# A state-space mixer with an MLP gate: state at every token instead of every second one, D by diagonal products, half-row products, B transposed from HBM

## Chip, cores, metric

One core of a Trainium2 chip. The metric is the device time of one execution in microseconds (us): the median of the runs. Engines: TensorE (PE, its weight loads PEld), VectorE (DVE), ScalarE (ACT), GpSimd (POOL), and SyncE (SP), which issues transfers.

## The reference

The input x has 2048 tokens of 448 values. It is normalised, and the result goes two ways: a complex diagonal state-space layer (with a skip term D) and a normalised MLP with GELU. The MLP's result gates the first through SiLU. Cut to what matters:

```python
def _A_ref(x, Lambda_re, Lambda_im, B_re, B_im, C_re, C_im, log_dt, Dskip):
    dt = jnp.exp(log_dt)
    Lam_bar = jnp.exp(dt * Lam)
    B_bar = ((Lam_bar - 1.0) / Lam)[:, None] * Bmat
    Bu = jnp.einsum("bld,pd->blp", x + 0j, B_bar)
    for t in range(L):
        h = Lam_bar[None, :] * h + Bu[:, t, :]
    y = 2.0 * jnp.einsum("blp,dp->bld", hseq, Cmat).real + x * Dskip[None, None, :]
    return y
def _B_ref(x, w1, b1, w2, b2):
    y = _layernorm(x, axis=-1)
    h = _gelu(jnp.einsum("bsd,df->bsf", y, w1) + b1)
    return jnp.einsum("bsf,fd->bsd", h, w2) + b2
xn = _layernorm(x, axis=-1)
return x + _A_ref(xn, ...) * _silu(_B_ref(xn, ...))
```

L is 2048, the state has 448 complex values, the MLP 1792 hidden ones. Inputs and output are bf16.

## The kernel before

**Tiles.** The 2048 tokens are taken in four groups g of 512; a group has two blocks b of 256 tokens, and a block is held as 128 partitions with two tokens each (par 0 the even one, par 1 the odd one). Every group goes through the same steps.

**Norms.** `ln_stats`, `ln_scale` and `ln_apply` make two normalised copies (xn for the state-space layer, xm for the MLP); `xt` transposes them by DMA into `xnT` and `xn2T`, so that input dimensions lie on partitions.

**State, every second token.** The state is kept after each pair of tokens: NK = 256 steps a group. `bu` multiplies the transposed pair (896 inputs, seven chunks of 128) by `BT`, which holds B for the odd token and Lambda times B for the even one. `lb` builds Lambda times B from the loaded `Bn` (ACT or DVE scale, DVE combine), `bt` transposes the result by DMA. `ssm` then works on DVE: two products and an add with the sine and cosine table `WT` (lines 669 to 673) turn the complex recurrence into real scans (line 677, seven a group, decay R2 of two tokens); ACT copies the result to bf16 (`s_b`, 681 to 684); POOL carries the last state to the next group (`cur`, 691 to 703); two products and an add (705 to 709) turn the state back into `h_sb`. The state's tiles are three real, three imaginary and one mixed.

**Output tiles.** `ym` makes y. For the odd token: seven products of h with `CQ` (C times the input factor). For the even token: seven products of the state before the pair with `CZ` (C times Lambda times that factor) and four products of the input with `M0`, the direct matrix from x to y of the same token. `m0` multiplies `Bn` with `CQ` (631, 636), copies the result and adds D on its diagonal (644). For odd tokens D enters through `skip`, as `xd` (776) and `xr` (808). `cq` builds CQ and CZ with `combine` (590 to 593).

**MLP.** For group 0 `mm1_half` (746) multiplies whole 128-row chunks, the last padded with zeros and the bias row, 256 tokens at a time; for the other groups `mm1` (726) uses 64-row halves, so that two products share the array. ACT applies GELU (736, 752). `mm2` (760) makes the output, DVE adds b2 (763), ACT applies SiLU (764). Then DVE multiplies by the gate (810) and adds x (813), and SP stores the tile.

**Order.** Every step is a task in `Plan`; its dependencies come from the keys that it reads and writes. The order of all tasks is written out as a list of numbers and tags, `ORDER`; every engine runs its tasks in that order, one after another, and a wait stops all that stands behind it on that engine. Some tasks have two versions (`either`); those in the list `SECOND` take the second one. PSUM banks are fixed in the code.

Of the kernel before, what the change touches and what calls it, by code (L numbers as in the profile page):

```python
# [7 lines left out]
ACT = mybir.ActivationFunctionType  # L8
# [9 lines left out]
class Task:  # L18
# [3 lines left out]
    __slots__ = ("eng", "ins", "reads", "writes", "sem", "idx", "deps", "chain", "alts", "tag")  # L22

    def __init__(self, eng, ins, reads, writes, sem):
        self.eng, self.ins, self.reads, self.writes, self.sem = eng, ins, tuple(reads), tuple(writes), sem
        self.deps = set()
        self.chain = False
        self.tag = None
        self.alts = [(eng, ins)]

    def choose(self, k):
        self.eng, self.ins = self.alts[k]
        if self.sem in ENGS:
            self.sem = self.eng


class Plan:
# [4 lines left out]
    def __init__(self, nc):  # L42
        self.nc = nc
# [19 lines left out]

    def add(self, eng, ins, reads=(), writes=(), dur=0.2, lat=0.1, prio=0.0, sem=None, chain=False, table=None, mode=None):
# [3 lines left out]
        t.chain = chain  # L68
# [7 lines left out]
    def either(self, first, second, reads=(), writes=(), prio=0.0, chain=False):  # L76

        t = self.add(first[0], first[1], reads, writes, chain=chain)
        t.alts.append((second[0], second[1] if isinstance(second[1], list) else [second[1]]))
        return t  # L80

    def dma(self, eng, out_ap, in_ap, reads=(), writes=(), prio=0.0, nbytes=0, transpose=False, dur=0.45):
# [8 lines left out]
        return self.add(eng, fn, reads, writes, sem=sem)  # L91
# [20 lines left out]
    def emit(self):  # L112
# [5 lines left out]
        assert len(order) == len(set(order)) == len(self.tasks)  # L118
        done = {}
# [26 lines left out]

    def settle(self, names):
# [14 lines left out]
ST 0 18 22 10 88 1 19 16 23 15 20 2 21 11 3 9 27 12 26 24 8 17 14 13 25 5 7 6 89 4 28 90 96 91 29 45 30 97 92 98 93 31 46 47 94 99 48 63 103  # L162
95 32 53 100 49 54 101 50 102 33 51 52 114 64 44 106 65 55 38 108 116 56 105 115 39 107 57 109 40 117 58 118 41 120 42 119 36 110 122 34 121
111 37 144 124 35 104 123 43 60 112 62 125 59 B0 126 DH 72 113 67 B1 296 68 69 128 B2 70 127 300 298 73 B3 151 130 129 299 191 148 132 303
131 149 297 134 133 301 302 150 304 136 152 135 142 155 138 66 156 143 153 140 154 137 157 271 139 71 146 308 305 74 165 76 75 141 306 61
309 145 79 307 166 268 82 272 163 BF 83 77 310 86 169 164 181 158 277 269 159 401 180 400 270 170 167 398 147 160 274 W0 W1 W2 405 168 404
182 399 W3 171 280 402 403 183 161 406 172 H10 173 275 162 H11 192 278 184 281 356 174 H12 175 357 185 358 311 78 410 360 80 176 81 H13 361
312 411 229 407 412 408 362 230 409 501 502 H15 363 500 314 188 231 359 315 504 383 189 506 503 H16 232 505 507 508 H14 186 368 178 364 369
187 233 509 365 179 512 366 234 H21 513 177 237 316 H20 367 238 460 313 239 458 510 461 235 242 190 246 373 243 459 245 514 195 193 196 511
236 247 H24 244 H23 194 199 251 466 85 197 200 84 464 198 203 87 249 252 201 253 240 202 241 205 248 204 317 370 206 215 262 217 207 382 318  # L170
218 257 216 258 319 208 254 259 250 D0 263 255 260 209 320 371 256 264 321 210 219 221 D1 220 211 223 265 266 273 222 376 267 413 374 322
224 212 225 D2 326 276 213 227 226 379 325 279 228 214 D3 327 282 331 465 333 323 283 414 285 375 377 332 380 H26 415 334 467 H22 O00 335
470 324 484 462 471 328 289 330 284 416 339 329 286 340 463 261 341 342 H30 290 343 344 417 337 336 292 515 548 418 O01 345 H25 351 516 346
549 H31 485 347 287 348 468 288 293 349 H33 350 550 372 352 338 554 419 378 353 518 354 294 384 291 420 295 421 469 385 387 422 551 423 517
O10 555 388 574 391 389 424 519 428 386 427 475 392 429 437 394 435 425 520 472 426 390 430 436 431 521 432 476 473 481 522 438 O11 433 381
523 440 395 482 447 393 478 434 448 524 575 439 441 442 443 449 450 453 444 451 445 525 446 355 479 452 H32 526 454 H34 455 552 396 556 553
456 397 529 457 H36 557 H35 530 560 531 558 561 539 527 538 559 486 565 483 474 528 487 536 477 535 489 480 534 532 562 537 541 O20 566 533
540 493 488 542 563 544 567 490 564 568 491 494 492 543 545 496 569 546 571 570 O21 495 547 581 572 497 573 578 498 576 O30 499 577 582 579
583 580 584 585 593 589 586 594 595 587 588 590 591 596 592
""".split()]  # L180
SECOND = [int(k) if k.isdigit() else k for k in """
142 143 144 157 163 167 171 173 195 201 219 223 308 309 407 411 413 416 484 485 508 509 512 515 516 518 519 575 W0 W1 W2 595
""".split()]

# [10 lines left out]
def bass_recurrent_scan__ssm_conv_s5__mixer_channel_mlp__prompt_kernel(  # L195
# [14 lines left out]
    NB, NG, NF, NK = 8, 4, 14, 256  # L210
# [3 lines left out]
    with ExitStack() as es:  # L214
        def SB(name, shape, dtype=BF):
# [5 lines left out]
        iota = SB("iota", [128, NK], F32)  # L221
        sgn = SB("sgn", [128, 4], F32)
        cw = SB("cw", [128, 40, 4], F32)
# [3 lines left out]
        dcol = SB("dcol", [128, 8], F32)  # L227
        x_all = SB("x_all", [128, NB, 2, D])
        w1_sb = SB("w1_sb", [128, 4, F])
        w2_sb = SB("w2_sb", [128, NF, D])  # L230
        b1b = SB("b1b", [128, NF])
        b1f = SB("b1f", [128, NF], F32)
        Bn = SB("Bn", [128, 7, 896])
        BT = SB("BT", [128, 7, 7, 128])
        Cr = SB("Cr", [128, 7, D])
# [9 lines left out]
        o2 = SB("o2", [128, 4, D], F32)  # L245
        WT = SB("WT", [128, 4, 3, NK])
        xn_sb = SB("xn_sb", [128, 2, 896])
        xn2_sb = SB("xn2_sb", [128, 2, 1024])
        xnT = SB("xnT", [128, 2, 7, 256])
# [8 lines left out]
        pb = SB("pb", [128, 3, 2, NK])  # L258
        v_sb = SB("v_sb", [128, 4, 2, NK])
        s_f = SB("s_f", [128, 4, 2, NK], F32)  # L260
        s_b = SB("s_b", [128, 4, 2, NK])
        h_sb = SB("h_sb", [128, 2, 7, NK + 2])
        Cs = h_sb[0:112, 1, :, :].rearrange("p k c -> p (k c)")[:, 18:530]
# [8 lines left out]
        (LRE, LIM, LDT, DT, F1, A1, R1, R2, F2, DEN, RDEN, LR, LI, NLI, T0, T1, QR, QI, NQR, NQI, ZR, ZI, NZR, NZI,  # L272
         T2, ZT) = range(26)
# [4 lines left out]
        def pool(fn, reads=(), writes=(), dur=0.3, prio=0):  # L278
            kb.add("pool", fn, reads, writes, dur=dur, lat=0.15, prio=prio)

        def dve(fn, reads=(), writes=(), dur=0.2, prio=0):
            kb.add("dve", fn, reads, writes, dur=dur, lat=0.12, prio=prio)

        def act(fn, reads=(), writes=(), dur=0.6, prio=0, table=None):
            kb.add("act", fn, reads, writes, dur=dur, lat=0.2, prio=prio, table=table)

        def pe(fn, reads=(), writes=(), dur=0.2, prio=0):
            kb.add("pe", fn, reads, writes, dur=dur, lat=0.25, prio=prio)

        with nc.Block():  # L290

            S0 = -100
            kb.tag = "ST"
            dve(lambda e: e.memset(still[:], 0.0), [], ["still"], 0.1, S0)
            pool(lambda e: e.memset(ident[:], 1.0), [], ["ident"], 0.2, 3 * PINNED)
            pool(lambda e: e.affine_select(ident[:], ident[:], [[1, 128]], ALU.is_equal, 0.0, base=0,
                                           channel_multiplier=-1), ["ident"], ["ident"], 0.4, 3 * PINNED)
            pool(lambda e: e.memset(sgn[:], -1.0), [], ["sgn"], 0.1, S0)
            pool(lambda e: e.affine_select(sgn[:, 0:1], sgn[:, 0:1], [[0, 1]], ALU.is_ge, 1.0, base=63,
                                           channel_multiplier=-1), ["sgn"], ["sgn"], 0.2, S0)  # L300
            act(lambda e: e.preload_act_table_set("natural_log_exp_and_others"), [], ["warm"], 0.05, 5 * PINNED, "exp")
            pool(lambda e: e.iota(iota[:], [[1, NK]], base=0, channel_multiplier=0,
                                  allow_small_or_imprecise_dtypes=True), [], ["iota"], 0.6, S0)

            pool(lambda e: e.tensor_scalar(sgn[:, 1:2], sgn[:, 0:1], -TWO_PI, None, op0=ALU.mult), ["sgn"], ["sgn1"], 0.2, S0)
            pool(lambda e: e.tensor_scalar(sgn[:, 2:3], sgn[:, 0:1], TWO_PI, None, op0=ALU.mult), ["sgn"], ["sgn2"], 0.2, S0)
            pool(lambda e: e.memset(sgn[:, 3:4], math.pi / 2), ["sgn"], ["sgn3"], 0.1, S0)
            XN = ["xn0", "xn1"]
            XM = ["xm0", "xm1"]
            dve(lambda e: e.memset(vrows[:, 0:64], 0.0), [], ["vr"], 0.1, S0)  # L310
            dve(lambda e: e.memset(w1_sb[64:128, 3, :], 0.0), [], ["w1b"], 0.5, S0)
# [617 lines left out]
```

## Time and profile before

| | |
|---|---|
| median of 3 runs | 154.56 us (154.44 to 154.69) |
| profiled execution, first to last instruction (span) | 153.0 us |
| mean granted TensorE clock | 0.999 |
| busy: PE, DVE, ACT, POOL | 148.4, 122.0, 110.9, 34.8 us |
| HBM read and written | 6.20 MB, 1.84 MB |

The profile shows one execution. Its span leaves out what lies around the instructions, and the median of the runs is 1.56 us above it. A row of a group reads: line, engine, operation, output<-inputs, shapes, count | busy time, mean ns of one | idle time of the engine before it and what ended that. PE's group means contain the pipeline's latency; what a product costs in a stream is read from the chain of waits. Rows of the timeline give start, duration and line.

### The profile page before, as it was taken

To read this page: it belongs to the slowest core of one execution; us is meant where nothing else is said; L and a number is where in the kernel's file an instruction comes from. 1 tells how busy PE (TensorE), PEld (TensorE's weight loads), DVE (VectorE), ACT (ScalarE), POOL (GpSimd) and SP (SyncE) were. 2 spreads that over 40 slices of the span, in tenths; PEclk is the share of its full clock that TensorE was granted. 3 is DMA by queue.
4 is the path that set the end of the run, shared out by engine and by line. 5 is a ranking of instruction groups with operands and counts; after the bars stand their busy time and mean duration, and the time that the engine had idled before them with its cause. 6 is when DMAs were issued, how large, how long until landed. Compare 5 with 4: busy or idle time off the path is not lost.

```text
span 153.0 us, 2971 instructions
## 1 busy us (share of the span) xinstructions
PE 148.4 (97%) x1055; PEld 88.2 (58%) x1055; DVE 122.0 (80%) x262; ACT 110.9 (72%) x190; POOL 34.8 (23%) x115
## 2 busy tenths in 40 slices
PE   7899999999999999999999999999999999999992
PEld 2599965455555555665544456755666555555551
DVE  5785989998957999899898864494976972999564
ACT  3867769999959988699999999832294789661100
POOL 6467491073000060310004310210006000000241
PEclk9999999999999999999999999999999999999999
DMA  4999986999989770000020221131300100001022
GB/s 114 297 324 366 252 185 118 177 125 227 196 143 121 140 137 0 4 0 0 2 50 14 42 78 60 27 38 27 95 4 0 60 0 0 4 0 62 0 107 73
DMA packets 31512, 14.04 MB, mean 92 GB/s; under 512 B 25733, under 2 KB 31113, under 8 KB 31498
## 3 DMA queue, kind: packets, MB, share of 16 engines
q1 hardware_dynamic: 31344, 13.79, 40.1%
q8 instruction: 8, 0.13, 0.3%
q10 hardware_dynamic: 154, 0.07, 0.2%
q14 instruction: 6, 0.05, 0.1%
HBM read 6.20 MB, written 1.84 MB: 53 GB/s over the span
## 4 chain that ended last, share of the span: by engine, by line
PE 94%; DVE 2%; DMA 1%; issue 0%; DVEq 0%
PE psum L760 28%; PE psum L726 21%; PE psum L652 14%; PE psum L795 13%; PE psum L746 8%; PE psum L798 4%; PE psum L631 3%; DMA x_all<-in_A_x_dram 1%; PE psum L801 1%; DVE lnst L395 1%; PE psum L636 1%; PE psum L403 1%; PE psum L466 0%; DVE xn2T L407 0%; DVE t L810 0%
## 5 line engine op out<-in xcount | busy, mean ns | idle before, releaser
L760 PE MATMUL psum<-w_sb,gT 128*128 128x448 bf16 x224 | 44.5, 353 | 0.0
L726 PE MATMUL psum<-xn2T,w_sb 64*128 64x512 bf16 x294 | 33.5, 378 | 0.0
L760 PEld LDWEIGHTS psum<-w_sb,gT 128*128 128x128 bf16 x224 | 21.8, 98 | 19.5 <-issue 0.2
L736 ACT ACTIVATE gT<-psum,b1f 128x512 bf16<-128x512 f32 x42 | 25.9, 690 | 3.1 <-PE psum L726 3.1
L726 PEld LDWEIGHTS psum<-xn2T,w_sb 64*128 64x128 bf16 x294 | 15.6, 109 | 16.3 <-issue 2.3
L652 PE MATMUL psum<-xnT,BT 128*128 128x256 bf16 x196 | 24.1, 273 | 0.0
L652 PEld LDWEIGHTS psum<-xnT,BT 128*128 128x128 bf16 x196 | 18.5, 98 | 6.4 <-issue 3.1
L677 DVE TENSOR_TENSOR_SCAN s_f<-cw,cur,v_sb 128x256 f32<-128x256 f32 x21 | 15.1, 740 | 0.2
L451 ACT ACTIVATE xn_sb<-x_all,lnw 128x448 bf16<-128x448 bf16 (+1 forms) x21 | 13.4, 667 | 1.2 <-POOL lnw L428 1.2
L764 ACT ACTIVATE g_sb<-o 128x448 bf16<-128x448 f32 x16 | 8.9, 572 | 6.4 <-DVE o L763 6.2
L746 PE MATMUL psum<-xn2T,w_sb 128*128 128x256 bf16 x112 | 12.7, 273 | 0.4 <-DVE xn2T L407 0.4
L746 PEld LDWEIGHTS psum<-xn2T,w_sb 128*128 128x128 bf16 x112 | 11.9, 111 | 0.9 <-issue 0.8
L795 PE MATMUL psum<-CZ,h_sb 128*128 128x448 bf16 x56 | 11.9, 353 | 0.0
L810 DVE TENSOR_TENSOR t<-psum,g_sb 128x448 bf16<-128x448 f32 (+2 forms) x10 | 5.7, 574 | 7.6 <-PE psum L798 3.8
L656 ACT ACTIVATE u_sb<-psum 128x512 bf16<-128x512 f32 x12 | 7.1, 593 | 5.9 <-PE psum L652 5.8
L763 DVE TENSOR_TENSOR o<-psum,b2bc 128x448 f32<-128x448 f32 x16 | 9.7, 614 | 1.5 <-PE psum L760 1.5
L795 PE MATMUL psum<-CQ,h_sb 128*128 128x448 bf16 (+2 forms) x54 | 10.5, 332 | 0.0
L752 ACT ACTIVATE gT<-psum 128x512 bf16<-128x512 f32 x14 | 8.2, 593 | 3.2 <-PE psum L746 3.1
L381 DVE BATCH_NORM_STATS2 lnst<-x_all 128x6 f32<-128x448 bf16 x14 | 8.3, 610 | 0.6 <-DMA x_all<-in_A_x_dram 0.5
L590 ACT ACTIVATE tmp<-Cr,cw 128x448 f32<-128x448 bf16 (+1 forms) x12 | 7.9, 672 | 1.0 <-DVE CQ L593 0.9
L691 POOL TENSOR_TENSOR cwk<-s_f,ang 128x3 f32<-128x3 f32 x3 | 1.1, 352 | 32.6 <-DVE s_f L677 32.5
L795 PEld LDWEIGHTS psum<-CZ,h_sb 128*128 128x128 bf16 x56 | 5.4, 98 | 4.9 <-issue 0.4
(157 smaller groups left out, 212.0 us busy)
## 6 DMA issues: line engine op xcount, KB each, us to landing
out_dram<-tmp SPq DMA_DIRECT2D x7, 224.0 KB, 1.9
x_all<-in_A_x_dram SPq DMA_DIRECT2D x3, 448.0 KB, 4.5
w_sb<-in_B_w_dram SPq DMA_DIRECT2D x3, 448.0 KB, 6.6
w_sb<-in_B_w_dram SPq DMA_DIRECT2D x3, 384.0 KB, 4.6
Bn<-in_A_B_im_dram SPq DMA_DIRECT2D x1, 336.0 KB, 9.3
Bn<-in_A_B_re_dram SPq DMA_DIRECT2D x1, 336.0 KB, 9.8
x_all<-in_A_x_dram SPq DMA_DIRECT2D x2, 112.0 KB, 2.1
x_all<-in_A_x_dram SPq DMA_DIRECT2D x1, 224.0 KB, 3.7
```

The lines of the kernel that those rows point to most:

```text
L381: dve([lambda e, b=b, par=par, q=q: e.bn_stats(lnst[:, q, :], x_all[:, 2 * g + b, par, :])], [f"x{2 * g + b}"] + (["xmT0p1"] if (g, b) == ...
L451: ("act", [lambda e, o=o, i=i: e.activation(o, i, ACT.Identity, bias=nb, scale=rs) for o, i in pairs], 0.75, 0.2)]
L652: fns = [lambda e, r=r, m=m, d=d: e.matmul(psum[:, 4, r * NK:(r + 1) * NK], BT[:, m, d, :], xnT[:, gx, d, :], start=(d == 0), stop=(d == 6 ...
L677: dve(lambda e, i=i, ri=ri, init=init: e.tensor_tensor_scan(s_f[:, i, ri, :], col(R2, i).to_broadcast([128, NK]), v_sb[:, i, ri, :], init, ...
L726: return lambda e: e.matmul(psum[:, b0 + k, :], w1_sb[halves[h], d, fcol(2 * j + k)], rhs[halves[h], d, :, :], start=first and d == 0, sto ...
L736: act([lambda e, k=k: e.activation(gT[:, gb, 2 * j + k, :], psum[:, b0 + k, :], ACT.Gelu_apprx_tanh, bias=b1f[:, 2 * j + k:2 * j + k + 1]) ...
L746: fns = [lambda e, k=k, d=d: e.matmul(psum[:, banks[k], :].rearrange("p (r c) -> p r c", r=2)[:, :, cs], w1_sb[:, d, fcol(2 * j + k)], rhs ...
L752: act(lambda e: e.activation(gT[:, 0, 2 * j:2 * j + 2, :].rearrange("p k (r c) -> p k r c", r=2)[:, :, :, cs], psum[:, b0:b0 + 2, :].rearr ...
L760: fns = [lambda e, fi=fi: e.matmul(psum[:, bk, 0:D], gT[:, gb, fi, q * 128:(q + 1) * 128], w2_sb[:, fi, :], start=(fi == 0), stop=(fi == N ...
L763: dve(lambda e: e.tensor_tensor(o2[:, ob, :], psum[:, bk, 0:D], b2bc[:], ALU.add), [f"ps{bk}", "b2bc"], [f"oo{ob}"], 0.62, prio - 76)
L764: act(lambda e: e.activation(g_sb[:, gs, :], o2[:, ob, :], ACT.Silu), [f"oo{ob}"] + (["silu"] if g == 0 else []), [f"g{gs}"], 0.58, prio - ...
L795: fns = [lambda e, k=k: e.matmul(psum[:, bk, c0:c1], h_sb[:, hb, k, k0:k0 + 128], cm[:, k, c0:c1], start=(k == 0), stop=False) for k in ra ...
```

## The change

The state is kept at every token. NK becomes 512, the scans use the decay R1 of one token, and Lambda times B, CZ and M0 are gone with `lb`, `m0` and `skip`. A block's tokens are laid out as two runs r of 128 neighbours, and x and its normalised copies are padded to 512 columns (the last 64 twice), so that the input rows lie in two 64-row halves. `bu` and both forms of the first MLP product go through one function that issues 64-row products for two results in turn. D enters in `ym` by four products of the transposed input with diagonal tiles `DG`. B comes transposed from HBM (its last 64 columns by way of a small copy `Bs`). The bias b1 is transposed on PE from rows that ACT loads, and GELU takes it for group 0 too. The banks of PSUM are given by a list, `BANKS`, and the order is a new list. The add of x can run on DVE or POOL: by the new `SECOND` 13 of 17 such adds run on POOL (all of groups 0 to 2, one of group 3). The scaling for CQ runs on ACT alone, as does the absolute value of the table.

The core of the diff ("..." where lines are left out; `x_all[:, xa(...)]` is the new place of a token run):

```diff
-    NB, NG, NF, NK = 8, 4, 14, 256
+    NB, NG, NF, NK = 8, 4, 14, 512
...
-        CZ = SB("CZ", [128, 7, D])
-        M0 = SB("M0", [128, 4, D])
-        dbc = SB("dbc", [128, D])
-        xd = SB("xd", [128, 4, D])
-        xr = SB("xr", [128, 2, D], F32)
+        DG = SB("DG", [128, 4, 128])
...
+            for r in range(2):
+                ld("sp", x_all[:, xa(0, r), 0:D], dram_ap(A_x, r * 256 * D, [[D, 128], [1, D]]), [f"x0p{r}"], 114688)
+            ldw1(0)
+            ldx(1, 1)
...
+                for d in range(4):
+                    h = slice(0, 128) if d < 3 else slice(0, 64)
+                    n = 128 if d < 3 else 64
+                    pool(lambda e, d=d, h=h, n=n: e.tensor_scalar(DG[h, d, 0:n], ident[h, 0:n], dcol[h, d:d + 1], None, op0=ALU.mult),
+                         ["ident", "dcol", f"DG{d}"], [f"DG{d}"], 0.4)
...
+            def bt():
+                for k, (bm, row, n, at) in enumerate(((A_B_re, 0, 224, 0), (A_B_im, 0, 192, 512), (A_B_re, 224, 224, 224), (A_B_im, 192, 192, 704), (A_B_im, 384, 64, 448))):
+                    kb.dma("sp", BT[:, 0:3, at:at + n], dram_ap(bm, row * D, [[D, n], [1, 384]]), writes=[f"BT{k}"], nbytes=768 * n, transpose=True)
...
+                def half(k, d, h):
+                    first = h == k
+                    return lambda e: e.matmul(out(k), wt(k, d, halves[h]), rhs(k, d, halves[h]),
+                                              start=first and d == 0, stop=not first and d == 2)
+
+                own = [half(k, d, k) for d in range(4) for k in range(2)]
+                other = [half(k, d, 1 - k) for d in range(3) for k in (1, 0)]
+                kb.tag = tag
+                pe(own, rd, [bank.key], rows(4, n))
+                pe(other, rd, [bank.key], rows(3, n))
...
-                            s_f[:, i, ri, :], col(R2, i).to_broadcast([128, NK]), v_sb[:, i, ri, :], init, ALU.mult, ALU.add),
+                            s_f[:, i, ri, :], col(R1, i).to_broadcast([128, NK]), v_sb[:, i, ri, :], init, ALU.mult, ALU.add),
...
+                    fns = [lambda e, k=k: e.matmul(psum[:, bank.b, c0:c1], h_sb[:, hb, k, k0:k0 + 128], CQ[:, k, c0:c1], start=(k == 0), stop=(k == 6))
                            for k in range(7)]
+                    ds = [d for d in range(4) if c0 <= d * 128 < c1]
+                    fns[1:1] = [lambda e, d=d: e.matmul(psum[:, bank.b, d * 128:min(D, d * 128 + 128)], xnT[:, gx, r * 4 + d, xs], DG[:, d, 0:min(128, D - d * 128)],
+                                                        start=False, stop=False) for d in ds]
...
+                    on = [("dve", add, 0.15 + 0.25 * w / D), ("pool", add, 0.2 + 1.0 * w / D)]
+                    kb.either(*on, rd, [f"o{ob}_{r}_{c0}"])
```

The first transfers on SP are now, in the new order: the second run of block 0, the last piece of w1 (192 KB), the first run of block 0, block 1, and then the first piece of w1 (384 KB) and its last rows (loaded twice, into both halves). The order of the groups' work stays as before in its outline: the MLP of group 0 first, then input products, scans and MLP of the following groups side by side, output tiles as their states come.

More of the change, by code (lines that the diff above doesn't have):

```diff
@@ L145, in emit, with place @@
         self.settle(list(self.counts))
+    def place(self, order):
+        held = {b.key: b for b in self.banks}
+        for t in self.tasks:
+            for k in set(t.reads + t.writes):
+                if k in held:
+                    held[k].tasks.append(t)
+        for b, k in zip(self.banks, BANKS, strict=True):
+            b.b = k
+        now = {}
+        for t in order:
+            for k in t.writes:
+                b = held.get(k)
+                if b is None or now.get(b.b) is b:
+                    continue
+                for i in range(b.b, b.b + b.n):
+                    if i in now:
+                        t.deps.update(now[i].tasks)
+                    now[i] = b
     def settle(self, names):
@@ L166 @@
[L166 to L173, printed above, removed]
@@ L468, in xt @@
[L468 to L472 removed]
+                bank = kb.psum()
+                pe([lambda e, d=d: e.transpose(psh[:, bank.b, d * 128:(d + 1) * 128], src[:, b, d * 128:(d + 1) * 128],
+                                               ident[:, :]) for d in range(8)], [key, "ident"], [bank.key], rows(8))
@@ L831, in bass_recurrent_scan__ssm_conv_s5__mixer_channel_mlp__prompt_kernel @@
-            P = {"ln": -9, "bu": -8, "mm1": 0, "mm2": 5, "ym": 6}
-            def pr(k, g, x=0.0):
-                return P[k] + 10 * g + x
+                if r and not last:
+                    kb.dma("sp", dram_ap(out, off, [[D, 128], [256 * D, 2], [1, D]]), o_sb[:, ob, :].rearrange("p (r d) -> p r d", r=2),
+                           reads=[f"o{ob}_0_0", f"o{ob}_1_0", f"o{ob}_1_256"], writes=[f"out{g}{b}"], nbytes=229376)
+            idle = kb.psum()
+            kb.tag = "I0"
+            pe([lambda e: e.matmul(psum[:, idle.b, :], still[:, :], still[:, None, :].to_broadcast([128, 4, 128]), start=True, stop=True) for _ in range(8)],
+               ["still"], [idle.key], 3.4)
```

804 lines of the change are left out of this document (367 added, 437 removed).

## The prediction

> **What bounds the kernel now.** I read the page first: its busy times and slices.
>
> ```profile
> PE 148.4 (97%) x1055; PEld 88.2 (58%) x1055; DVE 122.0 (80%) x262; ACT 110.9 (72%) x190; POOL 34.8 (23%) x115
> PE   7899999999999999999999999999999999999992
> DVE  5785989998957999899898864494976972999564
> ```
>
> PE is full in every slice between the head and the tail; DVE is full in many slices up to the middle and has holes after it. A busy PE can still wait inside a group, so I read the chain of waits next: it names the work whose end set the next start.
>
> ```profile
> by line: PE psum L760 27.8%; PE psum L726 21.5%; PE psum L652 14.5%; PE psum L795 13.1%; PE psum L746 8.2%; PE psum L798 4.0%; PE psum L631 2.6%; DMA x_all<-in_A_x_dram 1.3%; PE psum L801 1.0%; DVE lnst L395 0.8%; PE psum L636 0.5%; PE psum
> ...
> 7.22 5.40 PE psum L746 x48
> 12.62 0.45 PE psum L466 x8
> ...
> 41.19 3.13 PE psum L726 x28
> ...
> 150.06 0.43 DVE t L810
> 150.59 0.42 DVE tmp L813
> ```
>
> From 7.22 to 150.06 us the chain stays on PE without a break: 142.8 us of products. So TensorE's own work bounds the kernel, with 7.2 us of head and 2.9 us of tail. The last row gives the tail behind DVE: it ends at 151.0 us of a span of 153.0, so 2.0 us go to the last store. The span is 153.0 us and the median of the runs 154.56; I add their difference, 1.56 us, to every span below.
>
> The chain's durations are also the true prices of products: 28 half-row products of 512 columns take 3.13 us (0.112 each), 48 full ones of 256 columns 5.40 us (0.112 each), eight of 128 columns 0.45 us (0.056 each).
>
> **The change, part by part: TensorE.** M0 is no longer built: L631 and L636, 3.1% of 153.0, go (-4.8 us). M0's products go too, L798 4.0% (-6.1). In their place each of the 16 output tiles gets four diagonal products of at most 128 columns: 64 x 0.056 = +3.6. The input product L652 (14.5%, 22.2 us) becomes 168 half-row products of 512 columns (18.8) and 56 of 256 columns, two of which share the array: 28 pairs x 0.112 = 3.1, together 21.9 (-0.3). The first MLP products of group 0, L746 (12.5 us), lose their padded rows: 98 pairs of half-row products of 256 columns x 0.112 = 11.0 (-1.5). Sum: -9.1 us.
>
> Here the pairs are the unknown, since no row has half rows with 256 columns. The weight loads must also run in pairs:
>
> ```profile
> L726 PEld LDWEIGHTS psum<-xn2T,w_sb 64*128 64x128 bf16 x294 | 15.6, 109 | 16.3 <-issue 2.3 <-ACT gT L736 0.6 <-ACT w_sb L851 0.4
> ```
>
> 294 loads of 109 ns would be 32 us one after another; they cover 15.6, so two do run at once. A pair then costs 0.112, as I took it; were they serial, a pair would cost 2 x 0.109 = 0.218 and 126 pairs 13.4 us more. The diagonal products could cost from 0.056 to a load's 0.109 each, +3.4 us at the worst; they are nearest to the eight of 0.056.
>
> The load order puts one weight piece before the second row block of x, and the first products need both halves of the last rows; I take 0.3 us later for the first product. A TensorE that never waits would give a span of 153.0 - 9.1 + 0.3 = 144.2.
>
> **VectorE: what it gains and loses.** Every step of the scan part now runs over 512 tokens in place of 256 pairs.
>
> ```profile
> L677 DVE TENSOR_TENSOR_SCAN s_f<-cw,cur,v_sb 128x256 f32<-128x256 f32 x21 | 15.1, 740 | 0.2
> L705 DVE TENSOR_TENSOR pa<-s_b,WT 128x1536 bf16<-128x1536 bf16 x4 | 3.8, 948 | 0.0
> L563 DVE SCALAR_TENSOR_TENSOR s_f<-iota,cw,s_f 128x256 f32<-128x256 f32 x4 | 1.7, 474 | 0.0
> L708 DVE TENSOR_TENSOR pa<-s_b,WT 128x512 bf16<-128x512 bf16 x4 | 1.7, 422 | 1.2 <-ACT s_b L684 1.2
> L566 DVE SCALAR_TENSOR_TENSOR s_f<-s_f 128x1024 f32<-128x1024 f32 x1 | 1.2, 1224 | 0.0
> L709 DVE TENSOR_TENSOR h_sb<-pa 128x256 bf16<-128x256 bf16 x4 | 1.2, 289 | 0.1
> ```
>
> From L708 to L705, 1024 more elements cost 0.526 us; so 1536 to 3072 elements cost 0.79 more, for 24 instructions +18.9. Eight of 512 elements go to 1024: 8 x 0.26 = +2.1; eight of 256 to 512, by L709 to L708: 8 x 0.13 = +1.1. The 28 scans have one length only. At least they grow by the slope of L563 to L566 (0.977 ns an element, 0.25 us: +7.0), at most they double (0.74: +20.7). I take off L563's fixed part of 0.22 and double the rest: 0.52 each, +14.6. The table's f32 steps grow by about 2.0, and L566 goes to ACT: +0.8. Added: 37.5 us.
>
> ```profile
> L593 DVE SCALAR_TENSOR_TENSOR Bn<-Bn,cw,tmp 128x448 bf16<-128x448 bf16 x7 | 4.7, 671 | 0.0
> L593 DVE SCALAR_TENSOR_TENSOR CZ<-Cr,cw,tmp 128x448 bf16<-128x448 bf16 x7 | 4.7, 679 | 0.0
> L591 DVE TENSOR_SCALAR tmp<-Bn,cw 128x448 f32<-128x448 bf16 (+1 forms) x4 | 1.8, 454 | 0.0
> L591 DVE TENSOR_SCALAR tmp<-Cr,cw 128x448 f32<-128x448 bf16 x4 | 1.8, 446 | 0.1
> L644 DVE SCALAR_TENSOR_TENSOR M<-ident,dcol,psum 128x128 bf16<-128x128 bf16 (+1 forms) x4 | 1.3, 332 | 1.0 <-ACT M L633 0.5 <-ACT M L638 0.4
> L776 DVE TENSOR_TENSOR xd<-xn_sb,dbc 128x448 bf16<-128x448 bf16 x7 | 2.7, 379 | 0.0
> L808 DVE TENSOR_TENSOR xr<-psum,xd 128x448 f32<-128x448 f32 x7 | 4.3, 611 | 2.9 <-PE psum L801 2.9
> L852 DVE COPY w_sb<-w_sb 64x512 bf16<-64x512 bf16 x3 | 0.9, 288 | 0.1
> L311 DVE MEMSET w_sb<- 64x896 uint32 x1 | 0.8, 805 | 0.2 <-issue 0.2
> L813 DVE TENSOR_TENSOR tmp<-t,x_all 128x448 bf16<-128x448 bf16 x15 | 6.3, 430 | 0.1
> L450 DVE TENSOR_SCALAR xn_sb<-x_all,lnw 128x64 bf16<-128x64 bf16 x6 | 1.8, 297 | 0.0
> ```
>
> All these go, but of L813's 15 adds two stay on DVE: by the new list of second choices 13 adds of x run on POOL. Removed: 24.8 without L813, and 13 x 0.43 minus 0.3 for a half tile that comes to DVE, 5.3: 30.1 us in 63 instructions. Durations overlap on DVE, so less is freed:
>
> ```profile
> 2.85 0.63 DVE L395 BATCH_NORM_STATS2 lnst<-x_all 128x6 f32<-128x448 bf16 x1 [0.42 <-DMA x_all<-in_A_x_dram]
> ...
> 13.10 0.69 DVE L472 COPY xn2T<-psum 128x1024 bf16<-128x1024 bf16 x1 [1.61 <-PE psum L466]
> ...
> 129.67 2.03 DVE L677 TENSOR_TENSOR_SCAN s_f<-cw,cur,v_sb 128x256 f32<-128x256 f32 x3
> ```
>
> Three scans of 0.740 take 2.03, so each begins 0.06 before the last one ends; with dependent ones I take 0.05, and 63 x 0.05 = 3.2 was never on the clock. DVE's busy time becomes 122.0 + 37.5 - (30.1 - 3.2) = 132.6 us.
>
> DVE is one queue, so its sum is a path: its first statistics at 2.85, waits of the head 2.2 (the 1.6 before L472 and an estimate of 0.6 for shorter ones), 132.6, the tail 2.0: 139.7, plus 2.0 as an estimate for waits on ACT's copies and on late products: 141.7. That is still below TensorE's 144.2.
>
> **The new collision: POOL's adds beside VectorE.** The trace has this case.
>
> ```profile
> 98.66 1.38 POOL L775 TENSOR_TENSOR xd<-xn_sb,dbc 128x448 bf16<-128x448 bf16 x1 [9.86 <-DVE xr L808]
> ...
> 144.62 1.09 POOL L775 TENSOR_TENSOR xr<-xd,g_sb 128x448 f32<-128x448 bf16 x1 [23.33 <-ACT g_sb L764]
> ```
> ```profile
> 99.18 1.10 DVE L813 TENSOR_TENSOR tmp<-t,x_all 128x448 bf16<-128x448 bf16 x1
> ...
> 145.39 0.80 DVE L810 TENSOR_TENSOR t<-xr,g_sb 128x448 bf16<-128x448 f32 x1
> ...
> 146.64 0.62 DVE L810 TENSOR_TENSOR t<-psum,g_sb 128x448 bf16<-128x448 f32 x1 [0.45 <-PE psum L798]
> ```
>
> The DVE add that began beside POOL's 1.38 took 1.10 and ended just after it; other adds take 0.38 when nothing is beside them, so it lost 0.72. The next, beside 1.09, lost 0.18 (0.80 against 0.62). In the new order most of POOL's 13 adds stand beside scans and wide products of two SBUF tensors. I take the mean loss, 0.45 each: +5.9. The ends are 0 and POOL's own 1.09, 14.2 together. On POOL itself the adds wait for their gated tiles, and behind them in its queue stand the products that carry a group's last state to the next group's scans; these have a group's time to spare, so I add nothing.
>
> The DVE path is then 141.7 + 5.9 = 147.6 us, above TensorE's 144.2: VectorE, not TensorE, sets the end, and the last state of group 3 comes about 3.4 us after TensorE could use it. What waits on it: the four output tiles of group 3, their gating and the last store.
>
> **The other engines.** ACT gains wider copies (u, s_b: twice the elements), two gelus in place of one for each tile of group 0, and the second halves of the tables; it loses the Bn and CZ scalings and the M0 copies. I estimate 122 us from 110.9, with at least 20 us of room beside DVE: no term. SP issues as many transposes (26), seven of B now from HBM or a small copy in place of the 7 of Bn, which saves the wait for LB; B is needed only after group 0's MLP, 20 us later: no term, up to 2 us if the transposes queue behind the late norm of group 0.
>
> Forecast: 147.6 + 1.56 = 149.1 us (149.16, taken as 149.1).
>
> **The rivals.**
> 1. TensorE stays full: POOL's adds fall into DVE's waits and cost nothing. For it: DVE's path without them, 141.7, is below 144.2. Against: only 2.5 us of room over the whole span. 144.2 + 1.56 = 145.8 us.
> 2. Slower: each POOL add stops VectorE for its whole length. 141.7 + 13 x 1.09 = 155.9, 157.4 us. It decides from a loss of 0.87 us an add, where the path reaches 153.0. For it: L813's 0.72 of a possible 0.86. Against: L810's 0.18, and adds that stand beside instructions that read PSUM (146.64, beside POOL's second one, took its usual 0.62). The Trainium skill (SBUF — State Buffer, section SBUF: two separate sides) says that the pair of ports that VectorE and GpSimd share is an exclusive lock held for the whole instruction, against DVE instructions with two SBUF inputs or in a two-port mode. By that rule this rival is the likely one; the L813 row agrees (0.72 lost), and the L810 row shows how little is lost where POOL is nearly done.
> 3. A cold TensorE. If the 3.4 us come as one wait, the clock may fall before the last tiles.
>
> ```profile
> 1.04 3.60 PE L837 MATMUL psum<-still 128*128 128x512 bf16 x8 [1.04 <-DVE still L294]
> ```
>
> At the start, eight products of 512 columns take 3.60 us, 0.45 each, twice the warm price. The last four tiles, about 6 us, would lose up to 3.4 us while it lasts: 152.5 us. The Trainium skill (TensorE: Matmul & The Clock Gate, section HAM oscillation) says that gaps of over some 3.4 us bring the half clock back; no row of before has such a gap.
> 4. Half rows of 256 columns don't share the array: 144.2 + 13.4 = 157.6, 159.2 us. The load row speaks against it.
>
> **How the numbers follow.** Chances: forecast 0.46 (own range 147.0 to 151.5, from a loss of 0.3 to 0.6 an add), TensorE full 0.22, the port rival 0.19, cold TensorE 0.06, half rows 0.03, something else late (B's transposes, ACT) 0.04. 0.2% of 154.56 is 0.3 us, about what a measurement of this kernel can tell from no change. Faster: 0.43 of the forecast, 0.22, 0.03 of the cold case, 0.02 of the rest, 0.70 in all. Slower: 0.02 of the forecast, 0.19, 0.02 of the cold case, 0.03, 0.01: 0.27. Same: what is left, 0.03. The range goes from 145.8 (TensorE full) to 156.3 (a loss of 1.0 an add: 141.7 + 13.0 + 1.56); it leaves out the half-row case, the upper half of the port rival and a little below 145.8, together under 0.2.
>
> **What would show it.** Right: DVE's busy time at 130 to 140 us and above 85% in every slice; PE near 140 with waits before group 3's output tiles; the chain of waits on DVE (scans, wide products) in the second half; wide products of 1.74 us, scans near 1.26; instructions beside POOL's adds longer by some 0.5. Wrong: scans above 1.4 or below 1.1; a chain that stays on PE to the end (rival 1); wide products of 2.5 us and more in number beside POOL's adds (rival 2); granted clock below 0.97 (rival 3); half-row products of group 0 above 0.075 each (rival 4).

## The result: slower by 7.7%, and the profile after

The changed kernel takes 168.74 us (median of 4 runs, 165.98 to 170.68), the kernel before 154.62 beside it: ratio 1.077, 95% interval 1.067 to 1.087. The forecast was 149.1, in a range of 145.8 to 156.3. Some executions lose a few us to a lower granted clock (and in one of a later kernel TensorE ran at half speed throughout), and the ratios are made without these, so a ratio can stand below what two medians give. By the ratio the changed kernel takes 166.5 us, 17.4 more than the forecast.

The page of the changed kernel's profile: busy times, then the slices of PE, DVE and the granted clock. This execution took 170.68 us, its span is 169.0.

```profile
PE 148.9 (88%) x1164; PEld 80.1 (47%) x1164; DVE 136.6 (81%) x195; ACT 123.7 (73%) x185; POOL 78.7 (47%) x119
PE   7736399999798999999499999999989999993892
DVE  2860069858599979989949999999998969999934
PEclk9999968999999999999969999999999999999579
```

DVE's total is near what was forecast, and from the second quarter on most of its slices are full, as they should be. But PE's third and fifth slices are 3s and DVE's fourth and fifth are zeros: between 12.7 and 21.1 us DVE does nothing. The clock is lower behind them (slice 6), and again behind holes of PE at slices 20 and 37. The scans, two of the wide products and POOL's adds (busy us, mean ns):

```profile
L707 DVE TENSOR_TENSOR_SCAN s_f<-cw,cur,v_sb 128x512 f32<-128x512 f32 x21 | 27.8, 1368 | 1.4 <-POOL cur L727 1.4
L707 DVE TENSOR_TENSOR_SCAN s_f<-cw,v_sb 128x512 f32<-128x512 f32 x7 | 8.1, 1207 | 0.0
L737 DVE TENSOR_TENSOR pa<-s_b,WT 128x3072 bf16<-128x3072 bf16 x4 | 8.0, 2007 | 0.0
L738 DVE TENSOR_TENSOR pb<-s_b,WT 128x3072 bf16<-128x3072 bf16 x4 | 7.0, 1746 | 0.0
L808 POOL TENSOR_TENSOR tmp<-t,x_all 128x448 bf16<-128x448 bf16 x13 | 20.8, 1607 | 31.9 <-DVE t L806 22.6 <-issue 9.3
```

The scans and the wide products have the sizes of the forecast (1.26 and 1.74 us), except where they stand beside POOL. POOL's adds take 1.61 us, not 1.09 to 1.38.

**The head.** PE's timeline of the changed kernel (start, duration, and in brackets what it waited for):

```profile
10.43 1.05 PE L665 MATMUL psum<-xn2T,w_sb 64*128 64x256 bf16 x8 [2.66 <-DVE lnw L484]
12.28 3.17 PE L665 MATMUL psum<-xn2T,w_sb 64*128 64x256 bf16 x28 [0.79 <-DMA w_sb<-in_B_w_dram]
16.72 1.72 PE L665 MATMUL psum<-xn2T,w_sb 64*128 64x256 bf16 x28 [1.28 <-DMA w_sb<-in_B_w_dram]
21.17 0.63 PE L665 MATMUL psum<-xn2T,w_sb 64*128 64x256 bf16 x8 [2.73 <-DMA w_sb<-in_B_w_dram]
...
30.87 3.39 PE L776 MATMUL psum<-w_sb,gT 128*128 128x448 bf16 x17
```

and DVE's, which waits for the transpose that stands on PE behind these products:

```profile
22.39 0.69 DVE L517 COPY xn2T<-psum 128x1024 bf16<-128x1024 bf16 x1 [10.75 <-PE psum L515]
```

PE waits for w1 three times; the wait before 10.43 is put down to a DVE step that these products do not read, so it was most likely w1 too. The second MLP product begins at 30.87 us; before, the same row stands at 20.01:

```profile
20.01 10.76 PE L760 MATMUL psum<-w_sb,gT 128*128 128x448 bf16 x56
```

The transfers' rate tells why (window 4 to 20 us; the last columns are granted clock, DMA share and GB/s), first before, then after:

```profile
4.00:20.00 16.00, 15.38 (x149) 14.19 (x148) 12.68 (x41) 12.04 (x27) 9.76 (x37) 1.00 1.01 304
```
```profile
4.00:20.00 16.00, 9.28 (x93) 6.36 (x91) 6.25 (x22) 7.41 (x22) 4.73 (x19) 1.00 0.55 150
```

The loads run at half the rate, with nearly half of the DMA engines' time idle (a share of 0.55). SP, which issues them, is slowed too: eight loads of w1 took it 4.54 us before, seven take 8.78 now (first before, then after):

```profile
2.18 4.54 SPq L90 DMA_DIRECT2D w_sb<-in_B_w_dram  x8
```
```profile
2.80 8.78 SPq L107 DMA_DIRECT2D w_sb<-in_B_w_dram  x7
```

What is new among them is the load of w1's last 64 rows: it fills both row halves in one transfer, its source `[[0, 2], [F, 64], [1, w]]` reads the rows twice, and its outermost dimension is 2.

### The profile page after: what moved, and what is told of

Same layout as the page of the kernel before. It is cut to its first block, busy times and chain, and to the rows that moved or that the text cites. A ratio compares the mean times of both kernels' runs of the same rounds, so it can differ in the third digit from the quotient of the medians.

```text
span 169.0 us, 3086 instructions
## 1 busy us (share of the span) xinstructions
PE 148.9 (88%) x1164; PEld 80.1 (47%) x1164; DVE 136.6 (81%) x195; ACT 123.7 (73%) x185; POOL 78.7 (47%) x119
## 5 line engine op out<-in xcount | busy, mean ns | idle before, releaser
L665 PE MATMUL psum<-xn2T,w_sb 64*128 64x512 bf16 (+1 forms) x490 | 50.0, 354 | 8.5 <-DMA w_sb<-in_B_w_dram 4.8
L665 PEld LDWEIGHTS psum<-xn2T,w_sb 64*128 64x128 bf16 x490 | 28.0, 113 | 27.5 <-issue 6.2
L808 POOL TENSOR_TENSOR tmp<-t,x_all 128x448 bf16<-128x448 bf16 x13 | 20.8, 1607 | 31.9 <-DVE t L806 22.6
L800 PE MATMUL psum<-CQ,h_sb 128*128 128x448 bf16 (+2 forms) x119 | 28.7, 382 | 5.3 <-DVE h_sb L741 3.0
L707 DVE TENSOR_TENSOR_SCAN s_f<-cw,cur,v_sb 128x512 f32<-128x512 f32 x21 | 27.8, 1368 | 1.4 <-POOL cur L727 1.4
L665 PE MATMUL psum<-xnT,BT 64*128 64x512 bf16 (+1 forms) x224 | 24.1, 350 | 1.9 <-DVE o L785 1.8
L766 ACT ACTIVATE gT<-psum,b1f 128x256 bf16<-128x256 f32 x28 | 11.1, 481 | 11.5 <-PE psum L665 11.5
L800 PEld LDWEIGHTS psum<-CQ,h_sb 128*128 128x128 bf16 x119 | 11.5, 108 | 15.4 <-DVE h_sb L741 3.8
L682 ACT ACTIVATE u_sb<-psum 128x1024 bf16<-128x1024 f32 x12 | 12.1, 1023 | 0.3 <-PE psum L665 0.2
L500 ACT ACTIVATE xn_sb<-x_all,lnw 128x512 bf16<-128x512 bf16 x15 | 12.2, 817 | 0.2
L731 POOL TENSOR_TENSOR cwk<-cwk,ang 128x1 f32<-128x1 f32 x3 | 5.3, 1754 | 11.5 <-ACT cwk L730 11.5
```

The costliest lines, as they stand in the source:

```text
L500: ("act", lambda e: e.activation(dst, src, ACT.Identity, bias=nb, scale=rs), 0.81)]
L665: return lambda e: e.matmul(out(k), wt(k, d, halves[h]), rhs(k, d, halves[h]), start=first and d == 0, stop=not first and d == 2)
L682: act(lambda e: e.activation(u_sb[:, i, :, :], psum[:, bank.b:bank.b + 2, :], ACT.Copy), [bank.key], [f"u{i}"], 1.02)
L707: dve(lambda e, i=i, ri=ri, init=init: e.tensor_tensor_scan(s_f[:, i, ri, :], col(R1, i).to_broadcast([128, NK]), v_sb[:, i, ri, :], init, ...
L766: act([lambda e, k=k: e.activation(gT[:, 0, 2 * j + k, :].rearrange("p (r c) -> p r c", r=2)[:, :, cs], psum[:, bank.b + k, :].rearrange(" ...
L800: fns = [lambda e, k=k: e.matmul(psum[:, bank.b, c0:c1], h_sb[:, hb, k, k0:k0 + 128], CQ[:, k, c0:c1], start=(k == 0), stop=(k == 6)) for ...
```

## The experiments

**1. The load of the last rows in plain form, and the old kernel with the new form.** e1_split:

```
-  ld("sp", w1_sb[:, 3, a:a + w], dram_ap(B_w1, 384 * F + a, [[0, 2], [F, 64], [1, w]]), [f"w1r_{c}"], ...)
+  ld("sp", w1_sb[0:64, 3, a:a + w], dram_ap(B_w1, 384 * F + a, [[F, 64], [1, w]]), [f"w1r_{c}"], ...)
+  ld("sp", w1_sb[64:128, 3, a:a + w], dram_ap(B_w1, 384 * F + a, [[F, 64], [1, w]]), [f"w1q_{c}"], ...)
```

> The last 64 rows of w1 are loaded by two plain loads of 64 rows each in place of one load whose source repeats the rows (an outermost dimension of 2 with step 0); all else as in the changed kernel. Theory A, the repeating form is slow and holds up the loads and SP behind it: the second MLP product starts near 21 us in place of 30.9, DMA moves over 250 GB/s from 4 to 16 us, and the time falls by 8 to 10 us to 158.5 to 161. Theory B, the head is late because the new order puts more loads and transposes ahead on SP: the second MLP product still starts after 28 us, the time stays within 2 us of 168.7.

Measured: 158.64 us (158.34 to 159.24), ratio 1.026 (1.023 to 1.030). That is theory A: 10.1 us come back by the medians and 7.8 by the ratios. The second MLP product starts at 22.73 us. From 4 to 16 us the rate is 234 GB/s, less than the 250 expected; from 4 to 20 us it is 249, and eleven loads of w1 take SP 6.60 us:

```profile
4.00:20.00 16.00, 14.22 (x207) 11.71 (x205) 11.18 (x32) 11.61 (x35) 4.75 (x19) 1.00 0.95 249
...
2.75 6.60 SPq L107 DMA_DIRECT2D w_sb<-in_B_w_dram  x11
...
22.73 10.75 PE L777 MATMUL psum<-w_sb,gT 128*128 128x448 bf16 x56 [0.84 <-DMA w_sb<-in_B_w_dram]
```

e4_before_rep, in the kernel before:

```
-  ld("sp", w1_sb[0:64, 3, a:a + w], dram_ap(B_w1, 384 * F + a, [[F, 64], [1, w]]), [f"w1r_{c}"], ...)
+  ld("sp", <spare columns of gT>,   dram_ap(B_w1, 384 * F + a, [[0, 2], [F, 64], [1, w]]), [f"w1r_{c}"], ...)
```

> The kernel before; its four loads of the last 64 rows of w1 take the repeating form into a spare place (the rows themselves are left out: zeros stand for them in the first MLP product). Theory A: the head becomes 6 to 10 us later, 160 to 165 us in place of 154.6. Theory B: within 1 us of 154.6.

Measured: 162.20 us, ratio 1.049 (1.046 to 1.052): +7.4 us by four loads alone, in a kernel with nothing else of the change. Is it the repeat, or the 2? e8_before_outer2 reads 128 different rows in two blocks:

```
-  dram_ap(B_w1, 384 * F + a, [[0, 2], [F, 64], [1, w]])
+  dram_ap(B_w1, a, [[128 * F, 2], [F, 64], [1, w]])
```

> The kernel before; its four loads of the last 64 rows of w1 load 128 different rows into a spare place, with a source of two blocks of 64 rows (an outermost dimension of 2, step 128 rows, no repeat; zeros stand for the last rows in the first MLP product). If an outermost dimension of 2 is what makes the load slow: 162, as with the repeating source. If reading the same rows twice is: within 1 us of 154.7.

Measured: 162.43 us, ratio 1.050 (1.048 to 1.051). The same loss without a repeat, so the outermost dimension of 2 makes the load slow, not the reading of the same rows. Nor is it the doubled bytes, which e1_split loads too, in two loads. In these two kernels the rate from 4 to 20 us is 184 and 189 GB/s against 304 before, and a part of the loss is the granted clock, 0.79 in this window, which falls behind PE's waits for the loads. The Trainium skill (DMA: Bandwidth & Descriptors, section Rules for kernel authors) states a rule for this: the slowest dimension of the access patterns sets how many of the 16 engines a transfer uses, so a leading dimension of c confines it to at most c, and it names the leading repeat as the example. The runs agree in the time and in the DMA share (0.55 in the changed kernel, 0.58 and 0.60 in these two, 1.01 before); no view here shows single DMA engines, so that it was two of them is the page's word.

**2. POOL's adds.** e2_split_dve is e1_split with the 13 numbers of the adds taken out of `SECOND`, e3_dve the changed kernel with the same edit.

> As the kernel with the plain loads, and in addition the 13 adds of x that run on POOL go back to DVE. If a POOL add stops DVE for its whole length (13 x 1.6 = 20.9 us taken, 13 x 0.41 = 5.3 given back on DVE): DVE's busy time falls by over 8 us and the time by 6 us or more against that kernel, to 153 to 154. If an add costs DVE the 0.45 of the prediction: DVE's busy time stays within 1.5 us and the time too.

> The changed kernel with its repeating loads, only the 13 adds back on DVE. If head and adds are two separate costs, the difference to the changed kernel is that between the two kernels with plain loads, within 1.5 us. If the late head hides it (DVE has room after a late start), the difference is under 1 us whatever the adds cost there.

Measured: e2_split_dve 157.40 us (155.32 to 158.75), ratio 1.008 (1.005 to 1.011) against 1.026: 2.8 us. e3_dve 164.28, ratio 1.060 (1.055 to 1.065) against 1.077: 2.6 us by the ratios. So the adds cost about the same with either head. DVE's busy time is 136.2 us in e1_split and in e2_split_dve, though the second has 13 more instructions. Its adds, and two rows that shrank (e1_split first, then e2_split_dve):

```profile
L809 DVE TENSOR_TENSOR tmp<-t,x_all 128x448 bf16<-128x448 bf16 (+2 forms) x4 | 1.3, 331 | 0.4 <-DMA out_dram<-tmp 0.3
L708 DVE TENSOR_TENSOR_SCAN s_f<-cw,cur,v_sb 128x512 f32<-128x512 f32 x21 | 27.8, 1364 | 1.4 <-POOL cur L728 1.4
L738 DVE TENSOR_TENSOR pa<-s_b,WT 128x3072 bf16<-128x3072 bf16 x4 | 8.0, 2007 | 0.0
```
```profile
L809 DVE TENSOR_TENSOR tmp<-t,x_all 128x448 bf16<-128x448 bf16 (+2 forms) x17 | 6.1, 369 | 0.2
L708 DVE TENSOR_TENSOR_SCAN s_f<-cw,cur,v_sb 128x512 f32<-128x512 f32 x21 | 25.8, 1267 | 0.0
L738 DVE TENSOR_TENSOR pa<-s_b,WT 128x3072 bf16<-128x3072 bf16 x4 | 7.0, 1745 | 0.0
```

The adds add 6.1 - 1.3 = 4.8 us to DVE and the others give 4.8 back: a POOL add took 4.8 / 13 = 0.37 us from DVE, near the 0.45 of the forecast and far from the whole add. Neither theory saw the time go: it fell with DVE's busy time unchanged. What fell is waiting: PE's for h at the end, from 3.01 to 0.44 us. h is 1.6 us earlier: 0.8 since group 3's scans begin earlier, where DVE's wait of 1.4 us for `cur` is gone, and 0.8 since the wide product L738 behind them takes 1.73 us and not 2.53 beside a POOL add. The rest of the shorter wait is no gain: PE itself comes 1.0 us later in this execution, with a granted clock of 0.50 from 78 to 80 us.

**3. POOL's diagonals.** In e1_split PE waits 3.31 us at 72.8 for DG, which POOL builds behind the small state products:

```profile
69.12 1.71 POOL L728 TENSOR_TENSOR cur<-cwk 128x3 f32<-128x3 f32 x1
70.80 0.63 POOL L734 TENSOR_TENSOR cwk<-s_f,ang 128x1 f32<-128x1 f32 x1
71.51 2.19 POOL L735 TENSOR_TENSOR cur<-cwk 128x1 f32<-128x1 f32 x1
73.68 2.36 POOL L594 TENSOR_SCALAR DG<-ident,dcol 128x128 bf16<-128x128 bf16 x2
```

e5_dg moves the numbers 75, 76, 77 (DG0 to DG2; only 76 and 77 were late) in `ORDER` to stand behind 73, ahead of `cur`; e6_dg_dve does the same with the adds on DVE.

> The kernel with plain loads (158.6), and POOL builds the diagonals DG0 to DG2 ahead of the products that carry the state, at about 50 us in place of 73.7 to 76.0; the 13 adds stay on POOL. Theory: POOL's late diagonals hold the first output tile and through it VectorE: TensorE's wait of 3.3 us and VectorE's wait of 2.2 us before its first gating go, and as VectorE has no other hole to the end the time falls by 2 to 3 us to 155.6 to 156.6. Rival: another wait (the state's products on POOL, h) takes their place: less than 0.7 us.

> The same with the 13 adds on DVE (the kernel with plain loads and adds on DVE, 156.0 in its undisturbed runs, plus early diagonals). Theory: the 3.3 us hole after which the granted clock fell to 0.87 goes, 152.8 to 154.2 in nearly every run. Rival: the adds on DVE bring the same 1.4 to 2.6 us whether there is a hole or not and the hole costs nothing: 155.5 to 156.5, with runs that still vary by 3 us.

Measured: e5_dg 158.48 us, ratio 1.024 (1.022 to 1.026), 0.2 us by the medians and 0.4 by the ratios: the rival's outcome. The waits at 76 are gone, and `cur` and h come 2.0 us earlier than in e1_split (127.46 in place of 129.48, 145.42 in place of 147.44), but DVE still waits 1.37 us for `cur` and PE 3.0 us for h. In the profiled execution 1.4 of the 2.0 us are lost again behind h: the granted clock is 0.50 from 148 to 150 us, and seven products that take 1.49 us in e1_split take up to 2.50:

```profile
148.00 2.50 PE L801 MATMUL psum<-CQ,h_sb 128*128 128x448 bf16 x7
```

e6_dg_dve, where PE waits at most 0.6 us for h: 154.69 us (154.04 to 155.71), ratio 0.999 (0.997 to 1.002), 1.3 us below e2_split_dve by the ratios and between its two expectations. So an early DG brings time here only together with the adds on DVE; that the clock behind the wait for h takes it back in every run of e5_dg is not shown. e9_late_dve puts only the five adds of groups 2 and 3 on DVE:

> Plain loads and early diagonals; the 8 adds of groups 0 and 1 on POOL, the 5 of groups 2 and 3 on DVE (158.5 with all 13 on POOL, 154.7 with all on DVE). If each POOL add costs the same wherever it stands: 8/13 of the 3.8 us stay, 157.0. If the cost is made late (the wait for the state on POOL ahead of group 3's scans, and adds of group 2 beside group 3's last products): under 155.6. If it is made early: over 158.

Measured: 157.59 us, ratio 1.018 (1.013 to 1.023): five of 13 adds give 0.9 of 3.8 us. Equal shares (157.0) lie within this interval, so whether the adds of groups 0 and 1 cost more each stays open. Its profile still has the wait of 1.37 us for `cur`, which stands in POOL's queue behind the adds of group 1, and a wait of 2.2 us for h.

**4. What is left: the two halves of DVE's queue.** In e6_dg_dve the slow loads and POOL's waits are gone, and it is still 5.6 us above the forecast. The windows before and behind DVE's first product with u of group 0 (the third pair of columns is DVE's), for the kernel before, e1_split and e6_dg_dve:

```profile
0.00:46.66 46.66, 45.00 (x353) 29.82 (x355) 37.89 (x115) 36.80 (x67) 19.61 (x75) 1.00 0.92 210
46.66:153.00 106.34, 103.37 (x706) 58.35 (x702) 84.12 (x148) 74.09 (x124) 15.21 (x40) 1.00 0.18 40
```
```profile
0.00:40.12 40.12, 36.10 (x353) 22.34 (x355) 28.30 (x83) 32.56 (x60) 13.03 (x59) 1.00 0.91 196
40.12:156.90 116.78, 105.31 (x815) 54.52 (x809) 107.87 (x113) 90.67 (x125) 65.92 (x61) 1.00 0.23 46
```
```profile
0.00:39.77 39.77, 35.53 (x349) 22.01 (x351) 28.24 (x82) 32.52 (x60) 12.35 (x58) 1.00 0.88 194
39.77:152.30 112.53, 106.31 (x819) 55.81 (x815) 107.54 (x126) 90.56 (x125) 40.46 (x49) 1.00 0.27 49
```

The change took 9.6 us of DVE's work out of the part before that product (37.9 to 28.3) and put 23.8 us into the part behind it (84.1 to 107.9). Before it DVE has 11.5 us of idle time in e6_dg_dve, and the product starts when ACT's copy of u is there (it waits 0.24 us for it), at the end of PE's chain; behind it DVE is busy 96% of the time. Two kernels test this. e10_chain first moves POOL's parameter steps and `mhalf` ahead of two small copies that wait for B until 25 us (numbers 50, 12, 53 to 56 ahead of 159), which takes a wait of 2.5 us from DVE's head:

> Plain loads, early diagonals, adds on DVE (154.7), and POOL's parameter chain and mhalf stand ahead of the two small copies of B's last columns that wait for their loads until about 25 us. If the chain's lateness (VectorE's 2.5 us wait for POOL at 25 us) is paid at the end: 152.2 to 153.8. If the head has room up to 40 us, where VectorE waits for the input products anyway: within 0.4 us of 154.7.

Measured: 154.50 us (12 runs), ratio 0.998 (0.996 to 1.000). The wait is gone and the time is not measurably less: the head has room. Then seven memsets of 640 elements that nobody reads are put on DVE, in e12_head7 ahead of its four waits in the first 40 us, in e13_late7 ahead of group 3's products with u:

```
+  for k in range(7):
+      kb.tag = f"M{k}"
+      dve(lambda e: e.memset(spare[:], 0.0), [], ["spare"], 0.67)
```

> The kernel with plain loads, early diagonals, adds on DVE and the parameter chain ahead (154.5), with seven idle memsets of 640 f32 elements (about 0.67 us each, 4.7 us in all) on DVE ahead of its four waits in the first 40 us. Theory: the product of u of group 0 cannot start before about 40.0 us whatever DVE did before, so head work on DVE is free (and what the change removed there bought nothing): within 1 us of 154.5. Rival, the prediction's one sum over DVE's whole queue: +4 to +4.7 us, 158.5 to 159.2.

> The same seven memsets, all of them ahead of group 3's products with u (about 119 us). Theory: from 40 us on DVE has no hole, so each us is paid in full: +4.2 to +5.5, 158.7 to 160.0. Rival, TensorE sets the end there: under +2.

Measured: e12_head7 154.41 us, ratio 0.998 (0.995 to 1.001), no difference from e10_chain. e13_late7 159.0 to 160.8 us, ratio 1.033 (1.028 to 1.039): +5.4 us. In e12_head7 the memsets (7 x 0.59 us, and three waits of 0.20 for the one before, 4.7 us) fill DVE's waits up to the product with u, which begins at 41.02 us without a wait, 1.0 later than in e10_chain's profile. The profiled execution is 1.0 us longer than that of e10_chain, but the ratios, each good to 0.5 us, show no cost. In e13_late7 all seven stand one behind another, 5.3 us in all, and are paid in full; its granted clock is 0.96 to 0.99 (0.98 to 1.00 in e12_head7), so a part of this may be clock. In e12_head7:

```profile
33.64 0.59 DVE L335 MEMSET spare<- 128x640 f32 x1
34.43 0.59 DVE L335 MEMSET spare<- 128x640 f32 x1 [0.20 <-DVE spare L335]
...
40.51 0.59 DVE L335 MEMSET spare<- 128x640 f32 x1
41.02 1.69 DVE L705 TENSOR_TENSOR pb<-u_sb,WT 128x3072 bf16<-128x3072 bf16 x1
...
0.00:40.00 40.00, 36.36 (x347) 23.22 (x349) 31.61 (x87) 32.14 (x60) 14.09 (x57) 1.00 0.93 194
```

**5. A version that beats both.** Where DVE is full, b2 can be added by a PE product (`one0` with `b2bc`, through `B2_PE`) in place of a DVE instruction of 0.61 us. e7_b2pe8 does so for tiles 6, 7, 9, 10, 12 to 15 on top of e6_dg_dve, e11_chain_b2pe4 for 9, 10, 12, 13 on top of e10_chain; the SiLU of such a tile, which now reads the PSUM bank, moves up in `ORDER` to where the add stood, and a memset that `one0` needs stands earlier.

> The same with b2 added in TensorE for 8 of the 16 tiles (a product of one0 with b2bc, 8 x 0.19 = 1.5 us more on PE) in place of a VectorE instruction each (8 x 0.61 = 4.9 us less). If VectorE sets the end: 3.5 to 4.9 us faster than with the diagonals early and the adds on DVE, 148.5 to 150. If TensorE is the bound once the holes are gone: at most 1 us faster, or slower by up to 1.5.

> The same with b2 added on TensorE for 4 tiles (two of group 2, two of group 3). With VectorE as the bound: 4 x 0.61 = 2.4 us less than the kernel with the chain ahead. With TensorE and VectorE level: between 0 and 1 us less.

Measured: e7_b2pe8 154.04 us, ratio 0.995 (0.993 to 0.997): only 0.7 us. In its profile PE waits 1.4 us for ACT at 89 us, and from there to the end the chain stays on PE: TensorE is the bound there, as the second expectation had it. e11_chain_b2pe4 153.06 us (152.42 to 153.48), ratio 0.988 (0.984 to 0.991): 1.4 us below e10_chain, between its two expectations, and 1.2% faster than the kernel before.

## Why the prediction was wrong, step by step

Three steps failed, by the ratios: the head was priced 0.3 us later, and the loads cost 7.8; POOL's small products and DG were priced at nothing, and POOL cost 4.2 where the forecast held 1.1; DVE's queue was one sum, and it took 6.4 us more. Together 17.3 of the 17.4 us.

**Right: TensorE's sum.** Forecast -9.1 us from 148.4. PE is busy 141.4 us in e1_split and 140.4 in e10_chain, with a forecast of 148.4 - 9.1 = 139.3. The half rows of 256 columns share the array: in e10_chain 50 of them take 3.12 us, 0.062 each (0.056 was taken; the fourth rival needs 0.11). The first rival, TensorE full to the end, is refuted: PE waits 3.0 us for h ahead of group 3's output tiles, as the forecast said it would. That the size is near its 3.4 is in part luck, since DVE's wait of 1.4 us for `cur` is in it, which the forecast had put at nothing.

**Right: DVE's prices and POOL's toll.** Scans 1.21 to 1.27 us where POOL leaves them alone (1.26 forecast), wide products 1.75 (1.74), DVE busy 136.6 against 132.6 + 5.9 = 138.5, a loss of 0.37 us an add against 0.45. One reading behind the 132.6 was off: three scans of 0.740 us in 2.03 overlap twice, by 0.095 each and not 0.06, and 0.05 was used. The second rival, the whole add, is refuted in its price. The rule of the Trainium skill (SBUF — State Buffer, section SBUF: two separate sides) that one side waits for the whole instruction of the other is borne out mostly from POOL's side: its adds take 1.61 us, and a one-column product takes 0.19 us or ends with the wide products beside it, 3.69 us here (e2_split_dve):

```profile
116.36 0.19 POOL L732 TENSOR_TENSOR cwk<-cwk,ang 128x1 f32<-128x1 f32 x1 [16.64 <-ACT cwk L731]
116.64 3.69 POOL L733 TENSOR_TENSOR cwk<-cwk,sgn 128x1 f32<-128x1 f32 x1
116.86 1.75 DVE L738 TENSOR_TENSOR pa<-s_b,WT 128x3072 bf16<-128x3072 bf16 x1
118.53 1.75 DVE L739 TENSOR_TENSOR pb<-s_b,WT 128x3072 bf16<-128x3072 bf16 x1
```

**Wrong: "0.3 us later for the first product" and "SP ... no term".** This was the largest error, 7.8 of the 17.4 us. With plain loads the first product starts at 7.91 us, 0.7 later than before. The prediction counted the loads and their order and did not look at the shape of one of them. The rule of the Trainium skill that is named in the first experiment (DMA: Bandwidth & Descriptors, section Rules for kernel authors) speaks against this load and was not weighed.

**Wrong: "DVE is one queue, so its sum is a path".** It is a path only while nothing stops it. The prediction let DVE start at 2.85 us, gave the head 2.2 us of waits and subtracted the removed work wherever it stood. In fact DVE's queue is cut at the first product with u, near 40 us, which PE and ACT set: 11.5 us of idle time in place of 5.1, 6.5 us too little. The part behind the cut alone is 39.8 + 107.5, and with 5.0 us of waits and tail 152.3 of span. The forecast's own terms, with the adds on DVE, give a span of 141.7 + 4.8 = 146.5, 5.8 us less than in this execution, which is 0.5 us quicker than the ratio's time. Its busy time, 132.6 + 4.8 = 137.4 against 135.8, was 1.6 us too high, its late waits and tail (4.0 against 5.0) 1.0 too low: 6.5 - 1.6 + 1.0 = 5.9, the same within rounding.

**Wrong in part: "these have a group's time to spare".** The products that carry the state, and DG behind them, were not priced beside DVE's wide products. With the adds on POOL and DG late, 1.026 against 0.999: 4.2 us, of which the forecast held 5.9 - 4.8 = 1.1.

**The third rival, in part.** Seven products of an output tile after the wait of 3.0 us for h, in the changed kernel and in e1_split:

```profile
156.76 0.56 PE L800 MATMUL psum<-CQ,h_sb 128*128 128x448 bf16 x1 [3.02 <-DVE h_sb L741]
...
157.50 2.80 PE L800 MATMUL psum<-CQ,h_sb 128*128 128x448 bf16 x7
```
```profile
147.44 0.36 PE L801 MATMUL psum<-CQ,h_sb 128*128 128x448 bf16 x1 [3.01 <-DVE h_sb L742]
...
147.84 1.49 PE L801 MATMUL psum<-CQ,h_sb 128*128 128x448 bf16 x7
```

A wait of the same length brought nearly twice the price for two tiles in one execution and none in the other: the granted clock is 0.50 from 156 to 162 us in the first and 1.00 from 147 to 151 in the second. Nor does it take a gap of the 3.4 us that the prediction quotes: the clock fell to 0.56 behind one of 2.18 us (changed kernel, at 84 us), and stayed at 1.00 behind one of 3.31 (e1_split, at 76). The sign that was set for this rival, a clock below 0.97, was met (0.960). It fits that runs of the changed kernel differ by up to 4.7 us (165.98 at a clock of 0.998 to 170.68 at 0.960), and that they agree within 1.1 us in e11_chain_b2pe4, whose late PE waits are under 0.7 us. It is not the cause of the loss, which is 11.4 us at the clock of 0.998. What decides when the clock falls was not tried.

## What to carry to other kernels

Cut an engine's queue where another engine's result starts it anew, and make a sum for each part: work taken from a part that waits anyway buys nothing, work put into a full part was paid in full here, and work taken out of it paid only until TensorE became the bound (1.4 of 2.4 us, then 0.7 of 4.9). Read the access pattern of every transfer that a change touches, not only its bytes and its place: an outermost dimension of 2 cost 7.4 to 7.8 us by four loads of 64 to 128 KB. Small instructions on POOL that stand beside wide ones on VectorE should be priced at the wide ones' length, and what others wait for should stand ahead of them.

## What the runs showed of the hardware that was not expected

- Four loads with an outermost dimension of 2 cut the transfers' rate from 249 to 150 GB/s in the window of 4 to 20 us and hold SP, which issues seven loads of w1 in 8.78 us against eleven in 6.60 (changed kernel against e1_split).
- A POOL product of one column takes 0.19 us or 3.69 us, by what VectorE runs beside it (L732 and L733 in e2_split_dve), while VectorE loses 0.37 us on average to a POOL add of 1.61.
- The granted clock after a wait of 3.0 us fell in one execution and held in another; it fell behind a wait of 2.18 us and held behind one of 3.31.
